# A fused attention and MLP block: the first MLP weight blocks loaded by rows, TensorE's opening matmuls reordered, one DMA issue held by a wait

## The chip, the cores and the metric

The kernel runs on one core of one Trainium2 chip. The metric is the device time of the whole kernel in microseconds (us). The engines are TensorE (PE in the profile, with its weight loads as PEld), VectorE (DVE), ScalarE (ACT), GpSimd (POOL) and SyncE (SP). Matmuls write to PSUM, which the kernel divides into eight banks of 128 partitions x 512 f32. DMAs are issued from SP's queue (q1 in the profile) and from ScalarE's queue (q10).

## The reference

With `x` of 2048 tokens x 640 (bf16), 32 heads of 20, and an MLP width of 1728:

```python
xn  = layernorm(x)                              # no gain, no bias, eps 1e-5
q, k, v = split(xn @ wqkv)                      # 640 -> 3*640
phi = lambda t: where(t > 0, t + 1, exp(t)) + 1e-6
kv  = einsum("bhsd,bhse->bhde", phi(k), v)
z   = einsum("bhsd->bhd", phi(k))
s   = (phi(q) @ kv / (phi(q) @ z + 1e-6)) @ wo  # linear attention
g   = silu(relu(xn @ w1) @ w2)                  # 640 -> 1728 -> 640
out = x + s * g
```

## The kernel before

Tokens are in 16 tiles of 128 (index t), grouped in fours into J = 4 blocks of 512 (index j). The width 640 is C = 5 chunks of 128 (index k or c). The MLP width 1728 is NF = 13 blocks of 128 (index f) and a rest of 64. `xnT` holds the normalised x transposed, channels on partitions: a matmul of the first layer takes a 128x128 block of `w1_sb` as its stationary operand and columns of `xnT` as its moving one, and sums over the five chunks k.

The order of the calls in the Python code is the order of each engine's instructions. A small scheduler (`Sched`) keeps, for every named resource such as `("w1", 0)`, `("xnT", t, c)` or `("ps", b)`, who wrote it last and who has read it since, and puts semaphore waits in front of an instruction or a DMA issue for what it reads or overwrites. `extra` adds a wait on a named earlier operation. Each DMA has a semaphore of its own. An engine works through its list in order, so a wait holds all that stands behind it on that engine.

The opening works on the first block of 512 tokens (j = 0) and on the first five blocks of w1, f = 0 to 4, whose sums stand in banks `HF` = 2 to 6. While x and w1 are on their way, `fill` (L354, called in L584) runs nine 512-column matmuls of a constant into bank 0; nobody reads their result. Then for each of the four token tiles:

- `T_mean(t)` (L418) sums a row of x into its mean, on VectorE for t = 0 and on ScalarE for t = 1, 2, 3.
- `center(t, c0, c1)` (L430) subtracts the mean on VectorE, for chunks c0 to c1-1. The scale by the standard deviation comes later, after the matmuls.
- `T_pe(t, c0, c1, b)` (L435) transposes these chunks on TensorE into bank b, one 128x128 matmul with the identity `ident` per chunk.
- `T_copy(E, ...)` (L443) copies them from PSUM to `xnT`, on ScalarE or VectorE.
- `H_first(t, fs, ks)` (L578) does the first-layer matmuls of tile t for the w1 blocks `fs` and the chunks `ks`, one 128-column matmul for each pair: 25 for a whole tile. Each writes 128 of the 512 columns of its bank. After the last tile (t = 3), `H_ev` has ScalarE read the whole bank with a Relu.

The opening thus has 9 fill matmuls, 20 transposes (5 for each tile) and 100 H matmuls, and then the K projection (`K_mm`, L458) begins, which needs the weights `wk`. Everything behind it is the main part: K, Q and first-layer blocks, then the attention products and the second layer.

The opening's loads are issued in this order. SP: x0, x2, w1 part 1, x3, then `wk` (waiting for `center(0, 2, 5)`, L589 and L598), then w1 part 2 (waiting for `center(2, ...)`, L602 and L604), x4, x5, w1 part 3, x6, x7, `wq`. ScalarE: x1, w1 part 0, both with no wait, ahead of its first activation. The parts of w1 are columns (L359): part 0 is f = 0 to 2 (480 KB), part 1 is f = 3 and 4 (320 KB), part 2 f = 5 to 8, part 3 the rest. `w1_part(f)` names the part that an H matmul waits for. The H matmuls that need part 1, f = 3 and 4 of tiles 0 and 1, are called after tile 2's transposes (L613 and L616).

GpSimd's first own operation is the memset of `onesM` (L344), which is read only by `z_col`, late in the kernel; `ident`, `mhalf` and `zacc` are made behind it.

Of the kernel before, what the change touches and what calls it, by code (L numbers as in the profile page):

```python
# [211 lines left out]
def bass_recurrent_scan__linear_attn_block__dense_activation_relu__prompt_kernel(  # L212
# [9 lines left out]
    Bb, S, D = A_x.shape  # L222
# [3 lines left out]
    FF = B_w1.shape[1]  # L226
    P = 128
# [110 lines left out]
    def w_load(dst, src, key, extra=(), E="SP"):  # L338
        dma(E, lambda eng: eng.dma_start(dst, src.rearrange("(c p) n -> p c n", p=P)), W=[key], extra=extra)
# [3 lines left out]
    cwide = nc.const_aps.tensor(1.0, [P, 512], bf)  # L343
    sc.op("POOL", lambda eng: eng.memset(onesM[:, :], 1.0), W=[("onesM",)])  # L344
    sc.op("POOL", lambda eng: eng.memset(ident[:], 0.0), W=[("ident",)])
# [12 lines left out]

    W1C = [0, 3 * P, 5 * P, 9 * P, FF]  # L359
    NP = len(W1C) - 1  # L360

    def w1_load(i, extra=(), E="SP"):
        w_load(w1_sb[:, :, W1C[i]:W1C[i + 1]], B_w1[:, W1C[i]:W1C[i + 1]], ("w1", i), extra, E)

    def w1_part(f):
        return [i for i in range(NP) if W1C[i] <= P * f < W1C[i + 1]][0]

    x_load(0)
    x_load(1, E="ACT")
    x_load(2)  # L370
    w1_load(0, E="ACT")
    w1_load(1)
    x_load(3)

# [74 lines left out]
    def xtk(t, cs=range(C)):  # L449
        return [("xnT", t, c) for c in cs]  # L450
# [73 lines left out]
    def Q_block(j, f):  # L524
# [3 lines left out]
        else:  # L528
# [13 lines left out]
              R=[("er_e", es), ("er_r", es)], W=[("pqT", j, f)])  # L542

    def H_mm(j, f, b, lo=0, hi=512, ks=range(C)):
        return sc.group("PE", [(lambda eng, k=k: eng.matmul(ps[b][:, lo:hi], lhsT=w1_sb[:, k, P * f:P * (f + 1)],  # L545
                                                            rhs=xnT[:, k, 512 * j + lo:512 * j + hi],
                                                            start=(k == 0), stop=(k == C - 1))) for k in ks],
                        R=[("w1", w1_part(f))] + [kk for q in range(lo // P, hi // P) for kk in xtk(4 * j + q, ks)],
                        W=[("ps", b)])
# [11 lines left out]
    def H_halves():  # L561
        bs = [nextb(), nextb()]
        fns = []
        for jp in range(2):
            for k in range(C):
                for u in range(2):
                    fns.append(lambda eng, jp=jp, k=k, u=u: eng.matmul(  # L567
                        ps[bs[jp]][64 * u:64 * (u + 1), :], lhsT=w1_sb[:, k, NF * P:FF],
                        rhs=xnT[:, k, schunk(2 * jp + u)], start=(k == 0), stop=(k == C - 1)))
        sc.group("PE", fns, R=[("w1", NP - 1)] + [kk for q in range(16) for kk in xtk(q)], W=[("ps", b) for b in bs])  # L570
        for jp in range(2):
            sc.op("ACT", lambda eng, jp=jp: eng.activation(out=hTl[:, jp, :], in_=ps[bs[jp]], func=ACTF.Relu),
                  R=[("ps", bs[jp])], W=[("hTl", jp)])
# [9 lines left out]

    fill(9)  # L584
    T_mean(0, "DVE")
    T_mean(1)
    center(0, 0, 2)
    T_pe(0, 0, 2, 7)
    held = center(0, 2, 5)  # L589
    T_pe(0, 2, 5, 1)  # L590
# [3 lines left out]
    T_pe(1, 0, 2, 0)  # L594
    T_pe(1, 2, 5, HF[4])
    T_copy("ACT", 1, 0, 2, 0)
    T_copy("DVE", 1, 2, 5, HF[4])
    w_load(wqk[:, :, D:2 * D], A_wqkv[:, D:2 * D], ("wk",), [held])  # L598
    H_first(0, (0, 1, 2), (0, 1))
    H_first(0, (0, 1, 2), (2, 3, 4))  # L600
    T_mean(2)
    held = center(2, 0, C)  # L602
    H_first(1, (0, 1, 2))
    w1_load(2, [held])  # L604
# [7 lines left out]
    T_mean(3)  # L612
    H_first(0, (3, 4))  # L613
    T_copy("DVE", 2, 0, C, 1)
    center(3, 0, C)
    H_first(1, (3, 4))  # L616
    H_first(2, (0,))
# [387 lines left out]
```

## Time and profile before

| | us |
|---|---|
| three runs | 221.46, 221.61, 224.27 |
| median | 221.61 |
| the profiled execution | 221.12 |
| its span, first to last instruction | 219.4 |
| around the span in that execution | 1.7 |

| engine | busy us | share of the span |
|---|---|---|
| DVE | 114.4 | 52% |
| ACT | 87.5 | 40% |
| POOL | 43.5 | 20% |

The profile is of one execution. In its rows the first number is the start in us from the first instruction, the second the time to the end of the last instruction of the row; "x5" is a count of merged instructions. A matmul's duration in the rows contains its pipeline, so a row of back-to-back matmuls is best read by the distance of their starts. In the view by stretches the first number behind the window is the stretch's length, and then comes each engine's busy time with its count of instructions, the granted TensorE clock, the mean busy share of the 16 DMA engines and what they moved in GB/s.

### The profile page before, as it was taken

What the parts mean: (1) busy time and instruction counts of PE and PEld (TensorE: products, weight loads), DVE (VectorE), ACT (ScalarE), POOL (GpSimd) and SP (SyncE); (2) the same over time, 40 slices, a digit from 0 to 9 for tenths busy, and PEclk for the clock granted to TensorE, in tenths of its full rate; (3) what the DMA queues carried; (4) which work ended last, traced back from release to release, by engine and by line L of the source; (5) the groups of instructions that cost most, each with busy time, mean ns of one, the idle gap of its engine ahead of it and who ended that gap; (6) DMA issues with size and microseconds to landing.
All of it is one profiled execution on the core that took longest, in us unless ns stands there. A gap on an engine that the chain in (4) does not pass through costs nothing.

```text
span 219.4 us, 3577 instructions
## 1 busy us (share of the span) xinstructions
PE 215.5 (98%) x1489; PEld 134.2 (61%) x1489; DVE 114.4 (52%) x196; ACT 87.5 (40%) x143; POOL 43.5 (20%) x66
## 2 busy tenths in 40 slices
PE   8999999999999999999999999999999999999994
PEld 2975654555545554444477778777767776777673
DVE  2778857789676999987700007503322222314053
ACT  4587765576656575555421114531021102110300
POOL 2153101279024998600000000000000000000001
PEclk9999999999999999999999999999999999999999
DMA  6996581350012206800079968377110110000002
GB/s 212 300 382 155 127 225 57 71 45 6 0 30 60 33 1 121 167 3 0 0 228 362 261 202 326 93 241 269 60 63 1 60 33 30 30 31 33 30 30 90
DMA packets 28812, 24.51 MB, mean 112 GB/s; under 512 B 11812, under 2 KB 28156, under 8 KB 28796
## 3 DMA queue, kind: packets, MB, share of 16 engines
q1 hardware_dynamic: 27852, 23.53, 37.6%
q10 hardware_dynamic: 944, 0.75, 1.1%
q8 instruction: 11, 0.18, 0.3%
q14 instruction: 5, 0.04, 0.1%
HBM read 15.75 MB, written 5.24 MB: 96 GB/s over the span
## 4 chain that ended last, share of the span: by engine, by line
PE 96%; DMA 1%; DVE 1%; issue 0%
PE psT L845 26%; PE psT L545 26%; PE psT L891 10%; PE psT L790 10%; PE psT L462 10%; PE psT L530 10%; DMA reg<-in_A_x_dram 1%; PE psT L861 1%; PE psT L567 1%; PE psT L801 1%; PE psT L812 1%; PE psT L437 1%; PE psT L648 1%; DVE ek L424 0%; DVE reg L906 0%; DVE reg L898 0%
## 5 line engine op out<-in xcount | busy, mean ns | idle before, releaser
L545 PE MATMUL psT<-reg 128*128 128x512 bf16 (+1 forms) x335 | 61.7, 331 | 0.0
L845 PE MATMUL psT<-reg,hT 128*128 128x320 bf16 x416 | 60.1, 299 | 0.0
L845 PEld LDWEIGHTS psT<-reg,hT 128*128 128x128 bf16 x416 | 40.4, 98 | 16.4 <-issue 1.1
L545 PEld LDWEIGHTS psT<-reg 128*128 128x128 bf16 x335 | 28.5, 98 | 25.6 <-issue 0.4
L913 DVE TENSOR_TENSOR reg<-psT,reg 128x640 bf16<-128x640 f32 x15 | 12.4, 825 | 54.0 <-PE psT L891 54.0
L552 ACT ACTIVATE hT<-psT 128x512 bf16<-128x512 f32 x52 | 30.7, 599 | 15.8 <-PE psT L545 15.7
L879 ACT ACTIVATE reg<-psT 128x640 bf16<-128x640 f32 (+1 forms) x13 | 8.4, 661 | 44.3 <-PE psT L845 24.9
L898 POOL TENSOR_TENSOR reg<-reg 128x256 bf16<-128x256 bf16 x1 | 0.7, 668 | 124.4 <-DVE reg L906 124.4
L530 PE MATMUL psT<-reg 128*128 128x512 bf16 x100 | 24.9, 379 | 0.0
L462 PE MATMUL psT<-reg 128*128 128x320 bf16 x160 | 24.2, 299 | 0.0
L471 POOL TENSOR_TENSOR zacc<-zacc,reg 128x640 f32<-128x640 f32 x16 | 23.7, 1484 | 1.9 <-DVE reg L505 1.0
L891 PE MATMUL psT<-reg,pqT 128*128 128x320 bf16 (+2 forms) x165 | 24.0, 295 | 0.0
L790 PE MATMUL psT<-reg 128*128 128x320 bf16 x160 | 21.9, 299 | 0.0
L462 PEld LDWEIGHTS psT<-reg 128*128 128x128 bf16 x160 | 15.5, 98 | 8.3 <-DVE ek L489 0.3
L891 PEld LDWEIGHTS psT<-reg,pqT 128*128 128x128 bf16 x165 | 16.0, 98 | 5.8
L790 PEld LDWEIGHTS psT<-reg 128*128 128x128 bf16 x160 | 15.7, 98 | 6.2
L540 DVE SCALAR_TENSOR_TENSOR pqT<-er 128x512 bf16<-128x512 bf16 x20 | 17.1, 854 | 0.7
L530 PEld LDWEIGHTS psT<-reg 128*128 128x128 bf16 x100 | 9.7, 98 | 11.6 <-DVE er L538 0.6
L537 ACT ACTIVATE er<-psT 128x512 bf16<-128x512 f32 x20 | 12.0, 598 | 8.9 <-PE psT L530 8.1
L538 DVE TENSOR_SCALAR er<-psT 128x512 bf16<-128x512 f32 x20 | 13.6, 678 | 3.1 <-ACT er L537 3.1
L395 DVE BATCH_NORM_STATS2 stats<-reg 128x6 f32<-128x320 bf16 x32 | 13.9, 477 | 1.0 <-DMA reg<-in_A_x_dram 1.0
L505 DVE TENSOR_TENSOR reg<-ek 128x640 bf16<-128x640 bf16 x16 | 13.5, 843 | 1.5 <-ACT ek L496 1.0
(63 smaller groups left out, 133.9 us busy)
## 6 DMA issues: line engine op xcount, KB each, us to landing
rscr<-rden SPq DMA_DIRECT2D x4, 640.0 KB, 10.7
reg<-rscr SPq DMA_DIRECT2D x5, 512.0 KB, 6.1
reg<-in_A_x_dram SPq DMA_DIRECT2D x4, 640.0 KB, 6.9
reg<-in_A_x_dram SPq DMA_DIRECT2D x15, 160.0 KB, 3.3
out_dram<-reg SPq DMA_DIRECT2D x15, 160.0 KB, 1.8
reg<-in_A_wqkv_dram SPq DMA_DIRECT2D x2, 800.0 KB, 6.6
reg<-in_B_w_dram SPq DMA_DIRECT2D x1, 1120.0 KB, 5.7
reg<-in_B_w_dram SPq DMA_DIRECT2D x1, 960.0 KB, 8.2
```

The lines of the kernel that those rows point to most:

```text
L395: sc.op("DVE", lambda eng, a=a: eng.bn_stats(stats[:, t, a, :], xv[:, HN * a:HN * (a + 1)]), R=[("xin", t % XR)], W=[("stats", t, a)])
L462: fns.append(lambda eng, a=a, k=k: eng.matmul(ps[b + a][:, 0:HN], lhsT=xnT[:, k, tok(t)], rhs=wqk[:, k, D + HN * a:D + HN * (a + 1)], star ...
L471: sc.op("POOL", lambda eng: eng.tensor_tensor(out=zacc[:, :], in0=zacc[:, :], in1=pk[:, t, :], op=ALU.add), R=[("zacc",), ("pk", t)], W=[( ...
L505: sc.op("DVE", lambda eng: eng.tensor_tensor(out=pk[:, t, :], in0=e_, in1=r_, op=ALU.add), R=[("ek_e", es), ("ek_r", es)], W=[("pk", t)])
L530: sc.group("PE", [(lambda eng, k=k: eng.matmul(ps[b], lhsT=wqk[:, k, P * f:P * (f + 1)], rhs=rhs(k), start=(k == 0), stop=(k == C - 1))) f ...
L538: sc.op("DVE", lambda eng: eng.tensor_scalar(out=r_, in0=ps[b], scalar1=0.0, scalar2=1e-6, op0=ALU.max, op1=ALU.add), R=[("ps", b), ("er_e ...
L540: sc.op("DVE", lambda eng: eng.scalar_tensor_tensor(out=pqT[:, f, schunk(j)], in0=e_, scalar=1.0, in1=r_, op0=ALU.min, op1=ALU.add), R=[(" ...
L545: return sc.group("PE", [(lambda eng, k=k: eng.matmul(ps[b][:, lo:hi], lhsT=w1_sb[:, k, P * f:P * (f + 1)], rhs=xnT[:, k, 512 * j + lo:512 ...
L552: sc.op("ACT", lambda eng: eng.activation(out=hT[:, f, schunk(j)], in_=ps[b], func=ACTF.Relu), R=[("ps", b)], W=[("hT", j, f)])
L790: fns.append(lambda eng, t=t, a=a: eng.matmul(ps[b + a][:, 0:HN], lhsT=xn[:, t, P * k:P * (k + 1)], rhs=pk[:, t, HN * a:HN * (a + 1)], sta ...
L845: sc.group("PE", [(lambda eng, f=f, n=n: eng.matmul(ps[b + n][:, 0:HN], lhsT=hT[:, f, tok(t)], rhs=w2_sb[:, f, HN * n:HN * (n + 1)], start ...
L891: sc.group("PE", [(lambda eng, c=c, pb=pb, lo=lo, hi=hi: eng.matmul(ps[pb][:, 0:hi - lo], lhsT=pqT[:, c, tok(t)], rhs=wf[:, c, lo:hi], sta ...
```

## The change

Four things are edited, all in the opening.

1. The parts of w1. The first five blocks of 128 columns are loaded in two parts by rows: part 0 is chunks k = 0 and 1 of all five blocks (320 KB, ScalarE's queue), part 1 is chunks 2 to 4 of them (480 KB, SP's queue). Old parts 2 and 3 stay as they are. A row of w1 is then read in runs of 640 elements instead of 384 and 256. `w1_keys` names the part by chunk.
2. The order of loads. SP: x0, x2, x3, w1 part 1, `wk` with no wait, then as before. ScalarE: x1 now waits for the memset of `onesM`, and w1 part 0 stands behind it.
3. The order of TensorE. After `T_pe(1, 0, 2)` come the ten H matmuls of tile 0 with chunks 0 and 1, then the last three transposes of tile 1 (into bank 7 instead of bank 6), the ten of tile 1 with chunks 0 and 1, the fifteen of tile 0 with chunks 2 to 4, tile 2's transposes, and the fifteen of tile 1 with chunks 2 to 4. From `H_first(2, (0,))` on the order is the old one. As now two token tiles of one bank are open at a time, only the first tile's first matmul of a bank carries the start flag and only the last tile's last one the stop flag.
4. The fill is eight matmuls of 512 columns and one of 256, instead of nine of 512.

The counts of transposes, H matmuls, copies and activations are the same, and the order on VectorE, ScalarE (but for the wait) and GpSimd too.

```diff
-    sc.op("POOL", lambda eng: eng.memset(onesM[:, :], 1.0), W=[("onesM",)])
+    made = sc.op("POOL", lambda eng: eng.memset(onesM[:, :], 1.0), W=[("onesM",)])
...
-    W1C = [0, 3 * P, 5 * P, 9 * P, FF]
-    NP = len(W1C) - 1
+    W1C = [0, 5 * P, 9 * P, FF]
+    W1R = 2

     def w1_load(i, extra=(), E="SP"):
-        w_load(w1_sb[:, :, W1C[i]:W1C[i + 1]], B_w1[:, W1C[i]:W1C[i + 1]], ("w1", i), extra, E)
-
-    def w1_part(f):
-        return [i for i in range(NP) if W1C[i] <= P * f < W1C[i + 1]][0]
+        k0, k1, n = [(0, W1R, 0), (W1R, C, 0), (0, C, 1), (0, C, 2)][i]
+        w_load(w1_sb[:, k0:k1, W1C[n]:W1C[n + 1]], B_w1[P * k0:P * k1, W1C[n]:W1C[n + 1]], ("w1", i), extra, E)
+
+    def w1_keys(f, ks):
+        if P * f < W1C[1]:
+            return [("w1", i) for i in sorted({int(k >= W1R) for k in ks})]
+        return [("w1", 2 if P * f < W1C[2] else 3)]

     x_load(0)
-    x_load(1, E="ACT")
+    x_load(1, [made], "ACT")
     x_load(2)
     w1_load(0, E="ACT")
+    x_load(3)
     w1_load(1)
-    x_load(3)
+    w_load(wqk[:, :, D:2 * D], A_wqkv[:, D:2 * D], ("wk",))
...
-                                                            start=(k == 0), stop=(k == C - 1))) for k in ks],
-                        R=[("w1", w1_part(f))] + [kk for q in range(lo // P, hi // P) for kk in xtk(4 * j + q, ks)],
+                                                            start=(k == 0 and lo == 0), stop=(k == C - 1 and hi == 512))) for k in ks],
+                        R=w1_keys(f, ks) + [kk for q in range(lo // P, hi // P) for kk in xtk(4 * j + q, ks)],
...
-    fill(9)
+    fill(8)
+    fill(1, 256)
     T_mean(0, "DVE")
     T_mean(1)
     center(0, 0, 2)
     T_pe(0, 0, 2, 7)
-    held = center(0, 2, 5)
+    center(0, 2, 5)
     T_pe(0, 2, 5, 1)
     T_copy("ACT", 0, 0, 2, 7)
     center(1, 0, C)
     T_copy("DVE", 0, 2, 5, 1)
     T_pe(1, 0, 2, 0)
-    T_pe(1, 2, 5, HF[4])
+    H_first(0, range(5), (0, 1))
     T_copy("ACT", 1, 0, 2, 0)
-    T_copy("DVE", 1, 2, 5, HF[4])
-    w_load(wqk[:, :, D:2 * D], A_wqkv[:, D:2 * D], ("wk",), [held])
-    H_first(0, (0, 1, 2), (0, 1))
-    H_first(0, (0, 1, 2), (2, 3, 4))
+    T_pe(1, 2, 5, 7)
+    T_copy("DVE", 1, 2, 5, 7)
+    H_first(1, range(5), (0, 1))
+    H_first(0, range(5), (2, 3, 4))
     T_mean(2)
     held = center(2, 0, C)
-    H_first(1, (0, 1, 2))
     w1_load(2, [held])
...
     T_pe(2, 0, C, 1)
     T_mean(3)
-    H_first(0, (3, 4))
     T_copy("DVE", 2, 0, C, 1)
     center(3, 0, C)
-    H_first(1, (3, 4))
+    H_first(1, range(5), (2, 3, 4))
     H_first(2, (0,))
```

More of the change, by code (lines that the diff above doesn't have):

```diff
@@ L569, in H_halves @@
                         rhs=xnT[:, k, schunk(2 * jp + u)], start=(k == 0), stop=(k == C - 1)))
-        sc.group("PE", fns, R=[("w1", NP - 1)] + [kk for q in range(16) for kk in xtk(q)], W=[("ps", b) for b in bs])
+        sc.group("PE", fns, R=[("w1", 3)] + [kk for q in range(16) for kk in xtk(q)], W=[("ps", b) for b in bs])
         for jp in range(2):
```

## The prediction

> **What bounds the kernel now.** I read the page first (busy times, the TensorE clock, the chain), then the chain of waits of the opening in order of time, then the timeline of the first 12 us engine by engine, and last the DMA traffic in stretches.
>
> ```profile
> PE 215.5 (98%) x1489; PEld 134.2 (61%) x1489; DVE 114.4 (52%) x196; ACT 87.5 (40%) x143; POOL 43.5 (20%) x66
> ...
> PE 96%; DMA 1%; DVE 1%; issue 0%
> ```
>
> TensorE is the bound: it holds 96% of the chain that ended last. So an edit of the opening is worth only TensorE's idle time there. The chain of waits shows where that is:
>
> ```profile
> 0.79 2.87 DMA reg<-in_A_x_dram
> 3.66 0.02 issue
> 3.69 0.84 DVE ek L424 x2
> 4.52 0.02 issue
> 4.55 0.30 DVE reg L431
> 4.85 0.05 issue
> 4.89 0.98 PE psT L437 x10
> 5.87 1.72 PE psT L545 x30
> 7.59 0.28 PE psT L437 x5
> ```
>
> The chain leads from x0's landing (0.79 + 2.87 = 3.66) over its mean and first centring to the first transpose at 4.89. From there it is TensorE alone. The ten transposes of tiles 0 and 1 take 0.98 us, while five of tile 2 take 0.28: ten back to back would take 0.56, so about 0.42 us of waiting stands between them. Behind them H matmuls follow with no gap (1.72 / 30 = 57 ns each). The change therefore plays for some 0.4 us of waits, plus what an earlier x0 brings, against new waits for w1.
>
> **The change part by part.** These rows, picked one by one from the timeline, carry the opening's times:
>
> ```profile
> 0.79 0.20 POOL L344 MEMSET onesM<- 128x128 bf16 x1 [0.29 <-POOLq L990]
> 0.80 0.40 ACTq L336 DMA_DIRECT2D reg<-in_A_x_dram  x1
> 0.83 4.00 PE L355 MATMUL psT<-const-bfloat16-1.0 128*128 128x512 bf16 x9 [0.83 <-PEq L990]
> 1.23 0.47 ACTq L339 DMA_DIRECT2D reg<-in_B_w_dram  x1
> 3.77 0.15 PEld L355 LDWEIGHTS psT<-const-bfloat16-1.0 128*128 128x128 bf16 x1 [0.28 <-issue]
> 3.88 0.74 ACT L420 ACTIVATE ek<-reg 128x640 bf16<-128x640 bf16 x1 [0.87 <-DMA reg<-in_A_x_dram]
> 4.52 0.19 ACT L420 ACTIVATION_READ_ACCUMULATOR ek<-reg 128x1 f32 x1
> 4.98 0.38 DVE L431 TENSOR_SCALAR reg<-reg,mean 128x640 bf16<-128x640 bf16 x1
> 5.25 0.38 ACT L444 ACTIVATE reg<-psT 128x256 bf16<-128x256 bf16 x1 [0.55 <-PE psT L437]
> 5.41 0.28 PEld L437 LDWEIGHTS psT<-ident,reg 128*128 128x128 bf16 x5
> 5.75 0.22 PE L545 MATMUL psT<-reg 128*128 128x128 bf16 x1
> 11.89 0.30 PE L462 MATMUL psT<-reg 128*128 128x320 bf16 x1
> ```
>
> *Fill.* Its matmuls start 0.43 us apart (0.15 of a weight load and the 0.28 idle before it); half of one less ends it 0.21 us earlier, at 4.62 instead of 4.83. That removes nothing unless the first transpose (4.89) comes earlier too, which hangs on x0.
>
> *ScalarE's wait.* The memset ends at 0.99; with the 0.04 us from a centring's end (4.85) to the transpose that it lets go (4.89), x1's issue moves from 0.80 to 1.03, or at worst by the 0.29 us that the memset itself waited, to about 1.28. I take 0.25. Behind it on ScalarE are w1 part 0's issue (1.23 to 1.48), the table load and the mean of tile 1. ScalarE sat idle for 0.87 us ahead of that mean, so the shift itself costs nothing; x1's landing moves by 0 to 0.25 us. The mean's result was there at 4.71 (4.52 + 0.19) and VectorE took it at 4.98, so a delay to 0.27 us is covered.
>
> What x0 gains was not to be seen directly; the nearest rows are each queue's packets, from 1.6 to 2.1 us and then from 2.1 to 2.8:
>
> ```profile
> q1 hardware_dynamic: 30, 0.04, 43.1%
> q10 hardware_dynamic: 3, 0.00, 3.1%
> ...
> q1 hardware_dynamic: 66, 0.08, 43.3%
> q10 hardware_dynamic: 51, 0.07, 39.1%
> ```
>
> In the first half microsecond of traffic ScalarE's queue (q10) took only 3 of 33 packets, then 51 of 117. So x0 hardly shared at first, and shared later. The bounds are 0 and 0.25 us; I take 0.15. The first transpose then starts at 4.74.
>
> *TensorE's order.* Of the ten transposes, seven now precede the first H matmul. It needs ScalarE's copy of tile 0 (before: 5.25 + 0.38 = 5.63; with the 0.15, about 5.5), the second transpose of tile 1 (starts 5.41 and 5.47 before; its centring starts at 4.98 or a little earlier), and w1 part 0. The first H matmul started at 5.75 before. Without w1 it would start at about 5.55.
>
> *w1 and the loads.* The DMA rows are these. By stretch:
>
> ```profile
> 0.00:5.20 5.20, 4.31 (x13) 1.42 (x14) 1.48 (x5) 2.11 (x3) 1.44 (x9) 1.00 0.65 205
> 0.00:6.40 6.40, 5.51 (x31) 2.46 (x32) 2.35 (x7) 3.16 (x6) 1.44 (x9) 1.00 0.75 231
> 3.60:6.00 2.40, 2.33 (x18) 1.01 (x17) 2.09 (x7) 1.47 (x4) 0.00 (x0) 1.00 1.11 356
> 8.00:8.80 0.80, 0.80 (x18) 0.80 (x16) 0.80 (x3) 0.00 (x0) 0.00 (x0) 1.00 1.06 395
> ```
>
> and by issue, with the landing of x3 in ScalarE's timeline:
>
> ```profile
> reg<-in_B_w_dram ACTq DMA_DIRECT2D x1, 480.0 KB, 4.4
> reg<-in_B_w_dram SPq DMA_DIRECT2D x1, 320.0 KB, 4.9
> 7.05 0.74 ACT L420 ACTIVATE ek<-reg 128x640 bf16<-128x640 bf16 x1 [0.21 <-DMA reg<-in_A_x_dram]
> ```
>
> By 6.4 us 231 x 6.4 = 1478 thousand bytes had moved. That is the four x tiles and 800 KB of w1 (1440 KB of 1024 bytes: 1475). The last of them in SP's queue, x3, let its reader go at 7.05, 0.65 us later. After the change the same bytes move, and w1 part 1 is the last: at the old rate it lands at 7.05 too. Its rows are longer now, as those of `wk` are, which was under way from 8.0 to 8.8, at 395 GB/s; the mix of 3.6 to 6.0 gave 356. At 395 the stretch of 3.6 to 6.4 shrinks by 0.28 us, and part 1 lands at 6.77. [...]
>
> Part 0 (320 KB) landed as 480 KB at 1.23 + 4.4 = 5.63 before. Now it is done when q10 has moved 480 KB with x1, and q1 as much beside it: 983 thousand bytes. At 5.2 us 1066 had moved (205 x 5.2), so at 356 GB/s this point is 0.23 us earlier, 4.97, and some 0.15 later for q10's later start. With a lag of 0.33 (the last bytes of the 480 KB at about 5.3, the landing at 5.63) to 0.65 it lands between 5.45 and 5.75. I take 5.6 for the first H matmul.
>
> *The sum.* Before, 110 matmuls (100 H, 10 transposes) lay between 5.75 and the first K matmul at 11.89: 55.8 ns each. Now 113 do, for three transposes moved behind, so K starts at 5.6 + 113 x 0.0558 = 11.91. Part 1 sets a second floor: 23 matmuls (10 H, 3 transposes, 10 H) come before its first reader, 90 after, so K starts no earlier than the landing + 90 x 0.0558 = 11.79 (6.77) to 12.07 (7.05). The later of the two: 11.91 to 12.07, against 11.89. I take 12.0, that is +0.1 us. The ends: first H at 5.45 and the early landing give 11.79 (-0.1); first H at 5.75 and the landing at 7.05 or, as the whole traffic may shift by ScalarE's 0.25 us, at 7.3, give 12.06 to 12.32 (+0.2 to +0.4). So the 0.42 us of waits is not won: the transposes' holes are filled with H work, but three transposes (0.17) move behind, and the first H matmul was held by other things nearly as long.
>
> Later waits of the opening:
>
> ```profile
> 6.87 0.39 DVE L431 TENSOR_SCALAR reg<-reg,mean 128x640 bf16<-128x640 bf16 x1 [0.61 <-ACT ek L420]
> 8.31 0.38 DVE L431 TENSOR_SCALAR reg<-reg,mean 128x640 bf16<-128x640 bf16 x1
> 9.04 0.32 PEld L437 LDWEIGHTS psT<-ident,reg 128*128 128x128 bf16 x5
> ```
>
> Tile 2 is centred by 7.26; TensorE asks for it after 38 matmuls, at 5.6 + 2.1 = 7.7: covered. Tile 3's centring ended at 8.69 and its transposes began at 9.04, with 25 H matmuls between the two tiles' transposes. Now 20 lie there, 0.28 us less, of 0.35 to spare: 0.07 stays, taken as nothing, at worst 0.1. `wk` (819 thousand bytes) now follows part 1 directly: at 356 GB/s it lands 2.3 us behind it, by 9.4 to 9.6, and K asks for it at 12.0. The loads queued on SP behind it (w1 part 2, x4 and on) wait for tile 2's centring as before and find an emptier queue; TensorE, back to back in the chain, waited for none of them. The bank changed for a transpose (7 for 6) is free since ScalarE's copy at 5.63. The start flags add no instruction, zero.
>
> **How this stands to the runs.** The profiled execution took 221.12, 219.4 of it the span; the median of three runs is 221.61, 0.5 higher. The forecast adds 0.1 to either: 221.2 for such an execution, 221.7 for the median.
>
> **The rivals.** *The clock comes late* (slower). Fill matmuls of 512 columns start 0.43 us apart; later ones of that width run
>
> ```profile
> 14.77 1.08 PE psT L545 x5
> ```
>
> 0.216 apart. So TensorE runs at half rate at first, though the granted clock reads 1.00 in every stretch above, and it had doubled by the five transposes at 5.41 (0.28 us for five). The doubling comes some 4.1 us after the first fill matmul. The change shortens the dense fill to 3.79 us and then has fewer matmuls (7, not 10) up to 5.6. If the doubling needs the dense stretch that is cut, TensorE goes on at half rate for about as long again, from 4.95 to 9.05, and the work of 5.6 to 9.05 takes twice its time: +1.7 us, 222.9 or 223.4 on the median. Against it: the dense stretch shrinks by only 5%. For it: one of three runs took 224.27, 2.7 above the median, of which there is no trace. It decides if the H matmuls at 5.6 stand 107 ns apart instead of 56. To go beyond 2% (4.4 us) the half rate would have to last 8.9 us. [...]
>
> *w1 part 1 comes late* (slower). If `wk`, `x3` and the shared queues push it to 8 us, K starts at 13.02: +1.1 us, 222.7. For it: it now gates TensorE at 6.9, where before the 320 KB that landed at 1.71 + 4.9 = 6.6 were asked for only after 7.65. Against it: `wk` stands behind it in the same queue.
>
> *The opening gets shorter* (faster). x0 gains the whole 0.25 us, part 0 is in by 5.35, and long rows pay from the start, so that part 1 lands at 6.5: K at 11.66 to 11.6, -0.3 us, 221.3.
>
> *ScalarE's wait brings nothing*, as x0 has the engines to itself early in any case: TensorE then idles for 0.27 us after the shorter fill, first H at 5.75, +0.2 us: inside the forecast's own ends.
>
> **How the numbers follow.** The forecast (-0.1 to +0.4) with the idle wait in it 0.69, shorter opening 0.11, late clock 0.10, late part 1 0.07, a half rate or a load so late that 4.4 us are lost 0.02, something not seen that gains as much 0.01. The time is 221.7. The range from 220.8 to 222.9 holds the first two, the late part 1, and, at its low end, a median as good as the profiled execution's 221.12 with 0.3 off; it leaves out most of the late clock. What a measurement of this kernel can tell from no change is about 2%, 4.4 us: faster than 217.2 nothing above reaches (0.01), slower than 226.0 is 0.02, within 0.97.
>
> **What would show it.** First transpose near 4.75 (0.15 for x0), first H matmul at 5.5 to 5.7 and before the third to fifth transposes of tile 1, a wait of TensorE of at most 0.3 us for w1 part 1 near 6.9, first K matmul at 11.8 to 12.3, no gap after it. Wrong would be: H matmuls of the opening 107 ns apart, part 1 landing after 7.3, a gap before tile 3's transposes above 0.1 us, or a first K matmul before 11.7.

## The result and the profile after

The changed kernel takes 223.07 us (median of 22 runs, 222.07 to 225.94) against 221.75 for the kernel before (22 runs, 221.12 to 224.27): ratio 1.0053, 95% interval 1.0031 to 1.0075. It is slower, by about half a per cent, and the interval lies above 1. (Here and below the medians hold all runs; the ratios leave disturbed ones out.) The profiled execution took 222.65 us with a span of 220.9 us, 1.5 us more than the 219.4 of before.

The page of the changed kernel gives the chain's shares:

```profile
PE 95%; DMA 3%; SPq 1%; DVE 0%; issue 0%
```

TensorE still holds nearly all of it; new is the DMA's 3%. The chain of waits of its opening in order of time (start, length, what) shows where:

```profile
0.79 0.40 SPq L336
1.19 0.06 issue
1.25 0.42 SPq L336
1.67 0.04 issue
1.71 0.43 SPq L336
2.14 0.04 issue
2.19 6.08 DMA reg<-in_B_w_dram
8.26 0.14 issue
8.40 1.00 PE psT L552 x15
```

Before, the chain led over x0 and its centring to the first transpose. Now it leads over three x issues on SP's queue to w1 part 1, issued at 2.19 and landed 6.08 us later, at 8.26. TensorE's timeline says the same from its side:

```profile
4.42 0.81 PE L443 MATMUL psT<-ident,reg 128*128 128x128 bf16 x7
6.08 0.72 PE L552 MATMUL psT<-reg 128*128 128x128 bf16 x10 [0.85 <-DMA reg<-in_B_w_dram]
6.63 0.33 PE L443 MATMUL psT<-ident,reg 128*128 128x128 bf16 x3
6.80 0.72 PE L552 MATMUL psT<-reg 128*128 128x128 bf16 x10
8.40 1.00 PE L552 MATMUL psT<-reg 128*128 128x128 bf16 x15 [0.87 <-DMA reg<-in_B_w_dram]
9.23 0.44 PE L443 MATMUL psT<-ident,reg 128*128 128x128 bf16 x5
9.51 1.28 PE L552 MATMUL psT<-reg 128*128 128x128 bf16 x20
10.63 0.44 PE L443 MATMUL psT<-ident,reg 128*128 128x128 bf16 x5
10.90 2.68 PE L552 MATMUL psT<-reg 128*128 128x128 bf16 x45
13.42 0.84 PE L468 MATMUL psT<-reg 128*128 128x320 bf16 x5
```

The first transpose comes 0.47 us earlier than before (4.42 against 4.89), but the first H matmul waits for w1 part 0 until 6.08 (before: 5.75), and 20 H matmuls later TensorE stands again until part 1 is there, at 8.40. From there to the first K matmul it does 90 matmuls without a gap: 8.40 + 90 x 0.0558 = 13.42. Before, K began at 11.89; the difference, 1.53 us, is the whole difference of the spans (1.5). The main part behind it did not change: from the first K matmul to the last instruction the trace has 207.5 us before and after, and 207.5 to 207.8 in all the profiles below.

Why the loads are late is in the windows (length; busy time of PE, PEld, DVE, ACT, POOL; granted clock; DMA share; GB/s). First the kernel before:

```profile
3.40:6.20 2.80, 2.73 (x23) 1.31 (x22) 2.29 (x7) 1.67 (x5) 0.00 (x0) 1.00 1.10 359
6.20:8.30 2.10, 2.10 (x41) 2.10 (x39) 0.85 (x3) 1.47 (x4) 0.00 (x0) 1.00 0.91 243
```

and the changed kernel:

```profile
0.00:6.40 6.40, 4.72 (x22) 1.92 (x23) 2.00 (x6) 3.60 (x8) 1.44 (x9) 1.00 0.69 207
3.40:6.20 2.80, 1.95 (x14) 0.79 (x13) 1.80 (x6) 2.15 (x6) 0.00 (x0) 1.00 0.96 278
6.20:8.30 2.10, 1.32 (x23) 1.15 (x21) 0.65 (x2) 0.99 (x4) 0.00 (x0) 1.00 1.04 380
```

From 3.4 to 6.2 us the DMA engines are shown busy for 96% of the time and move 278 GB/s; before it was 359. By 6.4 us 207 x 6.4 = 1325 thousand bytes have moved, where 1478 had before. The DMA issues of the first 4 us (KB each, us from issue to landing) give the two loads of w1:

```profile
reg<-in_B_w_dram SPq DMA_DIRECT2D x1, 480.0 KB, 6.1
reg<-in_B_w_dram ACTq DMA_DIRECT2D x1, 320.0 KB, 4.5
```

### The profile page after: what moved, and what is told of

The parts are those of the page before. It is cut to its first block, busy times and chain, and to the rows that moved or that the text cites. A ratio compares the mean times of both kernels' runs of the same rounds, so it can differ in the third digit from the quotient of the medians.

```text
span 220.9 us, 3577 instructions
## 1 busy us (share of the span) xinstructions
PE 215.3 (97%) x1489; PEld 134.2 (61%) x1489; DVE 114.3 (52%) x196; ACT 87.5 (40%) x143; POOL 43.5 (20%) x66
## 4 chain that ended last, share of the span: by engine, by line
PE 95%; DMA 3%; SPq 1%; DVE 0%; issue 0%
PE psT L851 26%; PE psT L552 25%; PE psT L897 10%; PE psT L796 10%; PE psT L468 10%; PE psT L536 10%; DMA reg<-in_B_w_dram 3%; PE psT L867 1%; PE psT L574 1%; PE psT L807 1%; PE psT L818 1%; SPq L336 1%; PE psT L654 1%; PE psT L443 0%; DVE reg L912 0%
```

## The experiments

Eighteen kernels were run, in five groups. The table is worked out from the traces and results of all of them. The trace has 16 landings for each of these loads, called its shares here; "first to last" is when the first and the last share of w1 part 0 and of part 1 landed in the profiled execution. "GB/s" and "long" are the DMA rate and the number of packets that took over 250 ns, both between 3.4 and 6.2 us (in the kernel before, most packets of that stretch took 27, 36 or 55 ns, for their 512, 768 or 1280 bytes). Times are medians of the runs in brackets; the ratio is to the kernel before, run on the same chip, whose medians in the five groups lay between 221.59 and 221.72.

```
                               part 0        part 1       GB/s long  median (n)    ratio [95%]
before                         5.08 to 5.62  6.05 to 6.57  359   0   221.75 (22)
changed                        4.60 to 5.94  6.53 to 8.26  278  16   223.07 (22)  1.0053 [1.0031, 1.0075]
e1 changed, wk held            4.72 to 6.96  6.72 to 8.19  300  17   225.15 (6)   1.0133 [1.0095, 1.0171]
e2 before, wk free             5.34 to 5.75  6.31 to 6.73  365   0   221.55 (12)  1.0002 [0.9987, 1.0017]
e3 changed, no ACT wait        4.56 to 5.09  6.49 to 8.16  289  11   222.51 (6)   1.0039 [1.0024, 1.0055]
e4 before, ACT wait            5.28 to 7.94  6.21 to 8.63  254   8   223.63 (6)   1.0084 [1.0054, 1.0113]
e5 rows and order alone        4.45 to 6.05  5.80 to 7.50  340   5   221.83 (10)  1.0002 [0.9976, 1.0027]
e6 before, x3 ahead            5.16 to 6.79  6.47 to 8.16  347   2   222.27 (10)  1.0011 [0.9984, 1.0038]
e7 before, one part            6.19 to 6.99  (none)        375   1   222.71 (10)  1.0053 [1.0020, 1.0087]
e8 before, part 0 0.46 later   5.24 to 8.15  6.07 to 8.36  274   7   225.36 (4)   1.0133 [1.0083, 1.0183]
f1 before, part 0 1.07 later   6.71 to 7.63  4.92 to 6.99  276   4   225.11 (4)   1.0171 [1.0128, 1.0213]
f2 before, parts together      5.93 to 6.70  4.55 to 5.33  365   2   222.48 (10)  1.0053 [1.0024, 1.0082]
f3 before, ACT wait, x3 ahead  5.79 to 9.18  6.73 to 9.51  262   9   225.88 (4)   1.0101 [1.0046, 1.0156]
f4 changed, no wait, x3 back   4.61 to 5.23  5.88 to 6.69  379   2   221.71 (10)  1.0004 [0.9979, 1.0029]
g1 changed, x3 back            4.66 to 6.28  5.82 to 6.81  359   6   223.44 (12)  1.0059 [1.0026, 1.0092]
g3 parts swap queues           4.11 to 5.03  5.63 to 7.79  328  10   222.68 (12)  1.0033 [1.0001, 1.0064]
g4 the same, no ACT wait       4.44 to 5.08  5.42 to 5.98  377   0   221.51 (12)  0.9993 [0.9975, 1.0012]
h1 changed, fill in the wait   4.59 to 6.15  6.60 to 7.90  267  19   222.69 (12)  1.0062 [1.0032, 1.0092]
h2 changed, old fill           4.63 to 7.12  6.69 to 8.07  264  15   222.72 (12)  1.0069 [1.0040, 1.0098]
h3 w1 on ScalarE's queue       3.94 to 4.39  5.74 to 6.25  391   0   222.07 (12)  1.0027 [1.0005, 1.0049]
```

**First group: is it `wk`, or ScalarE's wait?** The changed kernel with `wk` held back again until tile 1 is being worked on:

```diff
-    w_load(wqk[:, :, D:2 * D], A_wqkv[:, D:2 * D], ("wk",))
...
-    center(0, 2, 5)
+    held = center(0, 2, 5)
...
+    w_load(wqk[:, :, D:2 * D], A_wqkv[:, D:2 * D], ("wk",), [held])
```

> The changed kernel, with wk's load waiting for VectorE's second centring of tile 0 again. Theory A (wk, queued directly behind w1 part 1 with no wait, takes DMA time from it, although it stands behind it in the same queue): part 1 lands near 7.0 us instead of 8.29, the first K matmul starts at 12.0 to 12.3 instead of 13.42, and the time falls by about 1 us from the changed kernel's, to 221.8 to 222.2. Theory B (the w1 parts by rows are slow transfers themselves, at the 240 to 300 GB/s seen from 3.4 to 6.2 us): part 1 still lands after 7.7 us and the time stays at 222.7 or more.

Measured: 225.15 us, slower still, and part 1 lands at 8.19, so holding `wk` does not bring part 1 back. (Much of the extra time is the clock, see the fifth group; why part 0 comes a microsecond later than in the changed kernel's profile is not shown.) The kernel before with `wk` released as the change does it:

```diff
     x_load(3)
+    w_load(wqk[:, :, D:2 * D], A_wqkv[:, D:2 * D], ("wk",))
...
-    w_load(wqk[:, :, D:2 * D], A_wqkv[:, D:2 * D], ("wk",), [held])
```

> The kernel before, with wk's load issued directly behind x3 with no wait. Theory A: x3, the last in front of it, lands later than 7.05 us, near 8, tile 3 is centred about 1 us later and TensorE waits 0.5 us or more before tile 3's transposes; the time rises by 0.4 to 1.0 us over before. Theory B: x3 lands at 7.0 to 7.2, no wait, the time is that of before within 0.2 us.

Measured: 221.55 us, no difference. So the early `wk`, which stands behind everything that the opening waits for, is not the cause. Next, ScalarE's wait: taken out of the changed kernel,

```diff
-    x_load(1, [made], "ACT")
+    x_load(1, E="ACT")
```

> The changed kernel with x1's issue not waiting for the memset. Theory: the wait gave x0 its 0.47 us (sum started at 3.21 instead of 3.69). Without it x0 lands near 3.6 again, the first transpose is back at 4.8 to 4.9; as TensorE then waits for w1 anyway (the first H matmul at 6.08 in the changed kernel), the time changes by 0.2 us or less. Rival: ScalarE's wait also delays w1 part 0 on its queue, and without it both parts land about 0.25 us sooner and the time falls by 0.2 to 0.3 us.

and put into the kernel before (with `made` the memset, as in the change):

```diff
-    x_load(1, E="ACT")
+    x_load(1, [made], "ACT")
```

> The kernel before with x1's issue waiting for the memset. Theory: x0 lands 0.4 to 0.5 us sooner, its sum starts near 3.2, but nine fill matmuls run until 4.83, so the first transpose starts at 4.85 at best, and w1 part 0 (on ScalarE's queue, 0.2 us later) lets the first H matmul start no sooner than 5.7: the time is that of before within 0.2 us. Rival: the later w1 part 0 costs its whole delay, +0.2 to 0.4 us.

Without the wait the changed kernel takes 222.51 us; part 0's shares land within half a microsecond, but part 1 still at 8.16. With the wait, the kernel before takes 223.63 us: x1 and part 0 each go out only 0.22 us later (1.02 for 0.80, 1.45 for 1.23), yet part 0 lands at 7.94 instead of 5.62. Both expectations for this kernel had at most 0.4 us for it. Its TensorE timeline:

```profile
4.62 1.27 PE L437 MATMUL psT<-ident,reg 128*128 128x128 bf16 x10
8.08 3.36 PE L545 MATMUL psT<-reg 128*128 128x128 bf16 x30 [2.18 <-DMA reg<-in_B_w_dram]
```

TensorE waits 2.18 us for part 0, and then the 30 H matmuls take 3.36 us: 112 ns each, where the chain of before has 57. That is about half speed. Both costs return below.

**Second group: the other edits one by one.** The change's loads by rows, TensorE's order and the shorter fill alone (x3 behind part 1, `wk` held, no wait on ScalarE; against the changed kernel):

```diff
-    x_load(1, [made], "ACT")
+    x_load(1, E="ACT")
...
-    x_load(3)
     w1_load(1)
-    w_load(wqk[:, :, D:2 * D], A_wqkv[:, D:2 * D], ("wk",))
+    x_load(3)
...
+    w_load(wqk[:, :, D:2 * D], A_wqkv[:, D:2 * D], ("wk",), [held])
```

> Of the changed kernel only the two parts by rows and TensorE's order (and the shorter fill); ScalarE's wait, x3's place and wk's wait as before. The earlier runs: without ScalarE's wait part 0 landed at 5.09 us, yet part 1 still at 8.16; ScalarE's wait alone, on the kernel before, pushed part 0 (by columns) to 7.94. Theory R (the parts by rows, read by two queues at a time, make their packets stall): part 1 lands at 7.5 us or later, the time is 222.2 or more. Theory X (x3 ahead of part 1 is what does it): part 1 lands near 6.6, the first K matmul starts near 12.0, the time is 221.4 to 221.9.

Measured: 221.83 us, no difference over its ten runs. Its one profile (221.87 us) does have late shares, part 1's last at 7.50, and its first K matmul at 12.66: so such a lag can come without any of the moved issues too, and each row of the table is one execution. The kernel before with only x3 moved ahead of w1 part 1:

```diff
-    w1_load(1)
     x_load(3)
+    w1_load(1)
```

> The kernel before with x3's issue ahead of w1 part 1's (320 KB by columns), nothing else. Theory R: no stalls, part 1 lands at 6.9 to 7.2 us, in time for its reader at 7.65, and the time is that of before within 0.3 us. Theory X: part 0 or part 1 lands at 7.5 us or later and the time rises by 0.5 us or more.

Measured: 222.27 us, 0.6 above the median beside it, with an interval that still holds 1. The kernel before with the five blocks in a single load on ScalarE's queue (the later parts move up by one number), to see whether long rows or the second load matter:

```diff
-    W1C = [0, 3 * P, 5 * P, 9 * P, FF]
+    W1C = [0, 5 * P, 9 * P, FF]
...
-    w1_load(1)
```

> The kernel before with the first five w1 blocks in one load (800 KB, rows of 640 elements, all five chunks) on ScalarE's queue behind x1, x3 directly behind x2. Without stalls it is done when 1475 thousand bytes have moved, 6.4 us by the rate of before, and lands at 6.6 to 6.9 us; TensorE waits 0.9 to 1.2 us for it after its transposes. Theory of long rows (runs of 640 elements of w1 stall whichever way they are split): it lands at 7.5 us or later. Theory of the split (two queues inside w1 at a time are what stalls): it lands by 7.0, and so sooner than part 1 of the changed kernel at 8.29.

Measured: 222.71 us. Its load lands whole at 6.99, its shares within 0.8 us: late because all of it is one piece, not because shares lag. Last, a delay of part 0 alone, x1 left in place (`made` is GpSimd's identity here, 0.46 us later):

```diff
-    w1_load(0, E="ACT")
+    w1_load(0, [made], "ACT")
```

> The kernel before, with w1 part 0's issue waiting for GpSimd's identity (0.2 to 0.5 us later than 1.23) and x1's issue unmoved. In the run with x1's issue waiting for the first memset both were 0.22 us late and part 0 landed at 7.94 us instead of 5.63. Theory: it is part 0's place in time against x2 and part 1 on SP's queue that decides: it lands after 7 us here too, and the time rises by 1 us or more. Rival: it is x1's start, after x0 has had the engines alone: part 0 lands at 5.8 to 6.2 and the time rises by 0.1 to 0.5 us.

Measured: 225.36 us. In its profile a part 0 that goes out 0.46 us later lands 2.5 us later.

**Third group: overlap of issues, or the delay?** Part 0 held until a later constant of GpSimd (issue at 2.30), when SP has nearly finished issuing:

```diff
-    sc.op("POOL", lambda eng: eng.memset(zacc[:, :], 0.0), W=[("zacc",)])
+    made = sc.op("POOL", lambda eng: eng.memset(zacc[:, :], 0.0), W=[("zacc",)])
...
-    w1_load(0, E="ACT")
+    w1_load(0, [made], "ACT")
```

> The kernel before with w1 part 0's issue waiting for GpSimd's last opening memset (issue near 2.35 us instead of 1.23), so that SP issues part 1 (1.71 to 2.14) wholly ahead of it. Theory O (what hurts is that the two w1 parts are issued by the two queues at the same time: 1.23 against 1.71 was fine, 1.45 against 1.70 landed at 7.94, 1.69 against 1.70 at 8.15): here the two no longer overlap, the parts come one after the other, part 0 last: it lands at 6.6 to 7.2, the engines' shares within 0.8 us of each other, and the time is 222.3 to 223.2, less than the 225.36 of the smaller delay. Theory L (every delay of ScalarE's load makes it worse): part 0 lands after 8 us and the time is 224.5 or more.

Both parts of w1 issued at the same time, nothing delayed on ScalarE:

```diff
-    x_load(2)
     w1_load(0, E="ACT")
     w1_load(1)
+    x_load(2)
     x_load(3)
```

> The kernel before with no wait and no delay, but SP issuing x0, w1 part 1, x2, x3: part 1's issue then falls at 1.22 to 1.65, together with part 0's at 1.23 to 1.70. Theory O: the shares of part 0 land far apart (more than 1.2 us), the last after 7 us, and the time rises to 223.5 or more. Theory L: nothing is later than before, part 0 lands by 6.0 and the time is within 0.4 us of before.

Measured: 225.11 and 222.48 us. With both issued together the shares stay within 0.8 us, SP's load is in at 5.33 and ScalarE's at 6.70, and the loss is the smaller one. With the longer delay the loss is as large as with 0.46 us; there the shares of SP's part 1, which was not delayed, lie 2.07 us apart and those of part 0 0.92. Neither theory has its landings right in either run. So two w1 loads issued at once do not by themselves make shares lag, while a later issue on ScalarE's queue went with a lag of one load or the other in e4, e8 and f1; the delayed issue of f1 still ran beside that of x3 on SP (2.18 to 2.70), so other overlaps are not excluded. The kernel before with ScalarE's wait and x3 ahead, and the changed kernel with neither:

```diff
-    x_load(1, E="ACT")
+    x_load(1, [made], "ACT")
...
-    w1_load(1)
     x_load(3)
+    w1_load(1)
```

> The kernel before with x1's issue waiting for the memset (so part 0's issue at 1.45 to 1.90) and x3 ahead of part 1 (so part 1's issue at 2.19 to 2.62): the wait without the overlap, by columns. Theory O: part 0 lands by 6.2 and the time is below the 223.63 of the wait alone, at 222.0 to 222.7. Theory L: part 0 lands after 7 us and the time is 223.3 or more.

```diff
-    x_load(1, [made], "ACT")
+    x_load(1, E="ACT")
...
-    x_load(3)
     w1_load(1)
+    x_load(3)
```

> The changed kernel without ScalarE's wait and with x3 behind w1 part 1 as before; wk issued with no wait behind x3. The parts by rows with TensorE's order alone gave 221.83 against 221.68 of before, so nothing, and wk's freedom alone 221.55, so nothing. If the edits add up, this takes 221.5 to 221.9; if wk directly behind takes time from part 1 or x3, 222.2 or more.

Measured: 225.88 and 221.71 us. The first has the loss without any of the row loads, the new order or `wk`; the second has all of these and no loss. So the loss of the change lies in ScalarE's wait and x3's place. (f3 has only four runs, and its ratio holds two of them.)

**Fourth group: which of the two, and by which load?** The changed kernel with x3 back behind part 1, the wait kept (against f4 it adds the wait alone):

```diff
-    x_load(3)
     w1_load(1)
+    x_load(3)
```

> The changed kernel with x3 behind w1 part 1 again, as before the change; ScalarE's wait stays. Theory D (every delay of the loads on ScalarE's queue costs more than the delay): the wait is the larger part of the loss, so this one loses most of what the change lost, 222.3 to 223.0 us, with the shares of w1 part 0 spread over more than 0.8 us. Rival X (x3 in front of w1 part 1 is what costs, the wait adds little by itself in this arrangement of w1): 221.5 to 222.0, w1 part 1 landed by 7.3 and the first K matmul at 12.0 to 12.3, or earlier for the earlier x0.

The changed kernel with the w1 loads on each other's queue, so that part 0 does not stand behind the wait, with and then without the wait:

```diff
-    x_load(2)
-    w1_load(0, E="ACT")
-    x_load(3)
-    w1_load(1)
+    w1_load(0)
+    w1_load(1, E="ACT")
+    x_load(2)
+    x_load(3)
```

> The changed kernel with the two loads of w1 on each other's queue: w1 part 0 on SP behind x0 (issue near 1.23, not delayed by ScalarE's wait), w1 part 1 on ScalarE behind x1 (issue near 1.44), then x2, x3 and wk on SP. ScalarE's wait for the memset stays, so x0 keeps its gain (first transpose near 4.4). Theory D with the delay of part 0 as the harm: part 0 lands near 5.2 to 5.6 and part 1 by 7.3, the first H matmul is at 5.3 to 5.7, K at 11.6 to 12.2, 221.0 to 221.8 us. Rival Q (what ScalarE's queue issues late lags, whatever it is): part 1 lands at 8 or later, K at 13 or later, 222.5 to 223.5. x2 goes out 0.4 later than before, and its tile is asked for near 7.4: a gap of up to 0.4 us there is possible under both.

> The kernel with the two w1 loads on each other's queue, without ScalarE's wait: x1 goes out at 0.80 and w1 part 1 at 1.23. Beside the run with the wait it prices the wait where w1 part 0 does not stand behind it. Theory D: without a delay on ScalarE's queue nothing lags, 221.3 to 221.9 us, first transpose back at 4.8 to 5.0. Rival Q: as ScalarE's load is not late here, 221.3 to 222.0 as well, so that the wait costs 1 us or more between the two runs, where theory D has 0 or a gain from the earlier x0. If both are slow (222.5 or more), the order of the loads itself costs, x2 and x3 behind w1 among it.

Measured: 223.44, 222.68 and 221.51 us. In the first, part 1 is in by 6.81, as the rival asked, and yet the loss is whole; part 0's shares lie 1.62 us apart, as theory D had it. The last two differ in the wait alone, and show it best. The DMA issues of the first 4 us and the window, with the wait:

```profile
reg<-in_A_x_dram SPq DMA_DIRECT2D x3, 160.0 KB, 6.1
reg<-in_B_w_dram ACTq DMA_DIRECT2D x1, 480.0 KB, 6.4
reg<-in_B_w_dram SPq DMA_DIRECT2D x1, 320.0 KB, 3.8
```

```profile
3.40:6.20 2.80, 2.80 (x24) 1.80 (x23) 1.76 (x6) 1.59 (x4) 0.00 (x0) 1.00 1.03 328
```

and without it:

```profile
reg<-in_A_x_dram SPq DMA_DIRECT2D x3, 160.0 KB, 4.7
reg<-in_B_w_dram ACTq DMA_DIRECT2D x1, 480.0 KB, 4.8
reg<-in_B_w_dram SPq DMA_DIRECT2D x1, 320.0 KB, 3.8
```

```profile
3.40:6.20 2.80, 2.52 (x16) 1.21 (x15) 2.00 (x6) 1.54 (x4) 0.00 (x0) 1.00 1.03 377
```

x1 and w1 part 1 go out 0.23 and 0.20 us later for the wait. Part 0 on SP takes 3.8 us from issue to landing either way; ScalarE's part 1 takes 1.6 us more. But the lag is not ScalarE's alone: the x loads on SP, which nobody delayed, take 6.1 instead of 4.7 at the median. So the rival of the expectation (what ScalarE's queue issues late lags, whatever it is) came closer, with K at 13.52 and part 1 in at 7.79, and "the delay of part 0 is the harm" fell; x0's gain of half a microsecond was kept and did not pay for it.

**Fifth group: the clock, and a try for a better version.** About half of the changed kernel's 22 runs (11) took 222.07 to 222.93 us, the rest 223.21 and more. The profile of g1 shows one way to the upper half:

```profile
4.68 0.94 PE L443 MATMUL psT<-ident,reg 128*128 128x128 bf16 x7
6.41 1.23 PE L552 MATMUL psT<-reg 128*128 128x128 bf16 x10 [0.79 <-DMA reg<-in_B_w_dram]
7.43 0.53 PE L443 MATMUL psT<-ident,reg 128*128 128x128 bf16 x3
7.75 2.42 PE L552 MATMUL psT<-reg 128*128 128x128 bf16 x25
```

Ten H matmuls take 1.23 us (0.72 in the changed kernel's profile). TensorE waits 0.79 us for part 0, and its matmuls start 107 ns apart until 9.56 and 56 ns behind that. (The granted clock in the windows reads 1.00 from 6.13 to 9.54 all the same, where 30 matmuls kept TensorE busy for 3.13 us, so the spacing has to be read.) To see whether the idle time does it, five fill matmuls were put into it:

```diff
     T_pe(1, 0, 2, 0)
+    fill(5, 256, 6)
     H_first(0, range(5), (0, 1))
```

> The changed kernel with five fill matmuls of 256 columns (into the bank that the first H group opens anew) between tile 1's first two transposes and the first H matmul, so that TensorE does not stand idle while it waits for w1 part 0. The loads are not touched. Theory C (part of the loss is the clock: where the idle time before the first H matmul falls into the 3.4 us that would have brought full speed, the opening runs on at half speed for 3.4 us more, +1.7 us): the upper of the changed kernel's two groups of times (223.2 to 224.6) goes, the median falls to 222.2 to 222.7, the granted clock reads full by 6.5 us and the H matmuls stand 56 ns apart. Rival L (the spread of the times comes from the loads' lag alone): the median stays at 222.8 to 223.4 with times above 223.2 in about half of the runs.

and the old fill was put back at the start:

```diff
-    fill(8)
-    fill(1, 256)
+    fill(9)
```

> The changed kernel with the old fill of nine matmuls of 512 columns. If the shorter fill is what lets the clock come late (the prediction's own rival), the upper group of times goes and the median falls to 222.2 to 222.7, less up to 0.2 us for a first transpose that now waits for the fill. By theory C (the idle time ahead of the first H matmul does it, not the fill's length) the median stays at 222.7 to 223.5 with both groups.

Measured: 222.69 us with 3 of 12 runs above 223.2, and 222.72 with 4 of 12. These two do not tell the theories apart: both medians lie at the edge between the ranges of the two expectations, and neither edit removes the upper times. Of theory C's 3.4 us the runs show the length of a stretch at half speed (e1: granted clock 0.50 from 7.91 to 11.32); that full speed would have come without the idle time was its author's guess. But the profile of h2 shows that the old fill does not protect the clock (windows as above; the granted clock is the third column from the end):

```profile
3.80:7.20 3.40, 1.40 (x10) 0.48 (x8) 1.38 (x6) 2.77 (x8) 0.00 (x0) 1.00 0.96 298
7.25:10.60 3.35, 3.35 (x32) 3.35 (x33) 0.65 (x2) 0.13 (x2) 0.00 (x0) 0.50 0.57 204
10.65:14.00 3.35, 3.35 (x63) 3.35 (x62) 2.52 (x7) 0.70 (x1) 0.56 (x2) 1.00 0.95 296
```

TensorE, waiting 2.06 us for part 0, was busy for 1.40 of 3.40 us; then the clock fell to 0.50, and 32 matmuls took the time of 63. The profiled executions with such a stretch have a mean clock of 0.991 (h2, f1), 0.992 (e1) and 0.985 (f3). It is 0.992 or less in 4 of the changed kernel's 22 runs, in 5 of 6 of e1, 3 of 4 of e8 and f3 and all 4 of f1, and in none of the runs of e2, e3, e5, e6, f4, g4 and h3: the kernels with the largest losses lose by the late load and by the clock behind it. Last, all x tiles on SP and both w1 loads on ScalarE's queue, each over 0.4 us earlier than before the change:

```diff
     x_load(0)
-    x_load(1, [made], "ACT")
-    x_load(2)
+    x_load(1)
     w1_load(0, E="ACT")
+    w1_load(1, E="ACT")
+    x_load(2)
     x_load(3)
-    w1_load(1)
```

> The changed kernel with all four first x tiles on SP and both loads of w1 on ScalarE's queue, without the wait: w1 part 0 goes out at 0.80 and part 1 at 1.23, each over 0.4 us earlier than before the change, x1 0.4 later. Theory D (a delay of what ScalarE's queue loads costs, nothing else does): no lag, 221.2 to 222.0 us; below 221.2 only if x0 gains from x1's later start, K at 11.5 to 11.9 then. Rival Q2 (SP's queue is served first and ScalarE's w1 loads starve behind four x tiles): part 1 lands after 7.5 and the time is 222.3 to 223.5.

Measured: 222.07 us, just above the first theory's range. The loads run at the best rate of all (391 GB/s, no long packet, w1 in by 6.25), so nothing starves on ScalarE's queue here; but x1, now behind x0 on SP, lands at 4.86, and TensorE waits for its centring until 6.19 (in this profile, of 223.62 us, 35 matmuls then take the 3.41 us from 6.55 to 9.96, and full speed first comes behind that). No version beats the kernel before beyond the uncertainty; g4, at 0.9993 (0.9975 to 1.0012), and f4 equal it.

## Why the prediction was wrong

The forecast was 221.7 us with a range to 222.9; 223.07 lies just above it. The step that failed is the price of two moves: of ScalarE's wait, taken as a plain shift of at most 0.25 us, and of x3's new place, taken as nothing. With the mean rate of before, that put part 1 at 7.05, or 7.3 at worst. It landed at 8.26, with the rate down and the shares of the loads apart. The case "w1 part 1 comes late" (8 us, K at 13.02, 222.7) is what the profiled execution shows, at 8.26 and 13.42; it had a chance of 0.07, and it named x3 and the shared queues among its reasons, but not ScalarE's wait.

- *TensorE is the bound and only the opening counts*: right. The span grew by what the first K matmul moved.
- *x1's issue*: put at 1.03, measured 1.02. *x0's gain*: taken as 0.15 us within 0 to 0.25; it was 0.48 (x0's sum began at 3.21 instead of 3.69). The step that bounded the gain by the delay was wrong: x0 gained twice the 0.22 us by which x1 was held. In g3 against g4 the first transpose gains the same 0.48 (4.41 against 4.89).
- *"The shift itself costs nothing"* of ScalarE's wait, with "some 0.15 later" for part 0: this failed. The step priced the wait as a plain shift of x1 and of part 0, with the first H matmul at 5.6; it came at 6.08. By the ratios of the table, the wait added to four kernels cost 0.55% (f4 to g1), 0.40% (g4 to g3) and 0.84% (before to e4), that is 0.9 to 1.9 us for 0.2 us of delay, and 0.14% (e3 to the changed kernel), which the intervals do not tell from nothing. What goes with it in the trace is not the delay but the lag: the rate from 3.4 to 6.2 us falls to between 254 and 328 GB/s in three of the four, and the last share of a w1 load comes 1.3 to 2.7 us behind its first in the changed kernel, g1, g3 and e4 alike.
- *"At the old rate it lands at 7.05"*, and 6.77 at the better rate: this is the same failure in the sum. By the sum's own terms the first H matmul at 6.08 would have put K at 6.08 + 113 x 0.0558 = 12.39; part 1 put it at 13.42. Landing at 8.26, part 1 missed the later of the two by 1.21 us. By 6.4 us 153 thousand bytes fewer had moved (1478 less 1325), 0.40 us at the 380 GB/s that followed; the remaining 0.8 is spread: the shares of part 1 came in from 6.53 to 8.26, where those of the last w1 load before came within 0.52 us of each other. Bytes alone did not hold it: from 6.4 to 8.26 us the engines moved 380 x 1.86 = 707 thousand bytes, while only 1475 - 1325 = 150 thousand of x and w1 were outstanding; the rest can only be `wk`, the one load issued behind part 1 by then. TensorE's wait ended only behind the last share (8.26, the next matmul at 8.40), and the sum had only bytes and a mean rate.
- *x3 ahead of part 1* had no price of its own, as "the same bytes move". Without the wait it costs 0.35% (0.8 us, f4 to e3), and part 1 lands at 8.16 instead of 6.69; with the wait it adds nothing (g1 1.0059, changed 1.0053). So with the parts by rows the two costs do not add up: either edit alone brings most of the loss. In the kernel before, x3's move alone is not told from nothing (e6).
- *`wk` behind part 1*: rightly taken as free (e1, e2, f4). Used as the argument against a late part 1 it was beside the point, since `wk` was not what could delay it.
- *Longer rows*: right in direction. Kernels without lag moved 375 to 391 GB/s by rows (f4, g4, h3, e7) and 359 to 365 by columns (before, e2, f2). Packets of 1280 bytes thus moved 3 to 9% more than a mix of 512 to 1280, which goes the way of the prediction's 395 against 356. The gain is worth nothing in time: f4 takes as long as the kernel before.
- *The floor*, K no earlier than part 1's landing + 90 x 0.0558: right (13.42 for a start at 8.40). *Tile 3*: covered, no gap ahead of its transposes.
- *The late clock* (0.10, +1.7 us): not in the profiled execution, whose H matmuls stand 56 ns apart, but in other kernels with late loads, and the shorter fill is not needed for it: full speed first came at 13.64 in e4, which has the old fill (35 matmuls in the 3.41 us from 10.23 on), the clock fell in h2 with the old fill, and f4 and g4, with the shorter one, lose nothing. Four of the changed kernel's 22 runs have a mean clock of 0.991 or 0.992; one stretch at half speed as in e1 (3.41 us) is 3.41 x 0.5 / 221 = 0.8%. What the other seven runs above 223.2 have is not shown: the profiled executions of g1 and h3, with a late first rise (9.56 and 9.96), have a mean clock of 0.999.

Not settled is why a load that ScalarE issues 0.2 us later, or a moved x3, makes some packets take over 250 ns (the changed kernel's 16 between 3.4 and 6.2 us took 258 to 813, where the others of their 1280 bytes mostly took 55). They stand on both queues: 10 of the changed kernel's 16 on SP's and all 11 of e3's, but 8 of f3's 9 on ScalarE's. The table shows that they go with the loss: every kernel with 7 or more such packets between 3.4 and 6.2 us lost 0.3% or more; of the four without any (before, e2, g4, h3) only h3 lost, held up by x1. Between them stand kernels of both kinds, and each profile is one execution of many: e5's has shares 1.6 and 1.7 us apart and its runs lose nothing on the mean. How often each kernel lags was not measured. And such packets are not a mark of the change alone: the kernel before has 18 of them from 6.2 to 9.0 us, where its TensorE waits for nothing. The trace doesn't name the engine of a packet, and no run was made that separates memory, engine and queue.

## What to carry to other kernels

A wait of 0.2 us on a queue that issues loads was not a shift of 0.2 us here (0.9 to 1.9 us in three of four kernels): price it with an experiment, and look at the last share of the load, not at bytes over the mean rate. The order and start times of the opening's loads were a setting found by trying; with ScalarE's loads 0.2 us later, the x loads on SP, which were not touched, took 6.1 us instead of 4.7 at the median (g3 against g4). A wait of TensorE early in the kernel cost more than its length in e4 (2.18 us, then 112 ns for a matmul), g1 (0.79 us, then 107) and h2 (2.06 us, then 105), where 56 to 57 was the usual spacing; in e8 a wait of 2.18 us was followed by 30 matmuls in 1.84 us.

## What the runs showed of the hardware

*Shares.* The 16 shares of w1 part 0 landed within 0.54 us of each other in the kernel before and 2.66 us apart with ScalarE's wait alone (e4). With both w1 loads issued at the same time (f2: 320 KB on SP, 480 KB on ScalarE's queue), SP's was in at 5.33 and ScalarE's at 6.70.

*Clock.* The record of the granted clock goes to full speed at 5.01 us in the kernel before and at 4.42 in the changed one, and to 0.50 behind the last instruction, at 220.05 and 222.88. TensorE was busy for 3.34 us from 1.60 to 5.01 (before) and for 3.41 from 1.01 to 4.42 (changed). Half speed lasted longer in three profiles, at a granted clock that read 1.00: in g1 30 matmuls kept TensorE busy for 3.13 us from 6.13 to 9.54, in h3 35 took 3.41 us from 6.55 to 9.96, in e4 35 took 3.41 us from 10.23 to 13.64; the next five transposes took 0.28 us up to the start of the matmul behind them, as in the kernel before. In four profiles the granted clock read 0.50 for a stretch: e1 from 7.91 to 11.32, h2 from 7.21 to 10.62, f1 from 7.27 to 10.68, f3 from 7.17 to 13.99. Just before, TensorE had been busy for 1.55 us from 4.49 to 7.91 (e1), 1.40 from 3.80 to 7.21 (h2), 1.54 from 3.85 to 7.27 (f1) and 1.59 from 3.75 to 7.17 (f3). In e8 it was busy for 1.44 us from 6.32 to 9.73, and the clock read 1.00 behind that, with 66 matmuls in 3.42 us. Each of these is one execution, and what makes the clock change is not shown.
